# A written order for the expert stage, and a block product accumulated on a copy of another

## The chip, the cores and the metric

One core of a Trainium2 chip runs the whole kernel. Times are device microseconds (us) of one execution. The median of three runs of the kernel before is 1386.89 us (1381.55 to 1387.7).

## The reference

Three layers follow one another; all data is float32.

```
attn:    q averaged over pairs of rows; softmax(q k^T / sqrt(64)) v;  2 x 8 heads, 1152 rows of k and v, 576 of q
gated:   x = (sigmoid(x @ w_gate) * (x @ w_val)) @ w_out            1152 tokens, 512 -> 1536 -> 512
experts: P = exp(x @ w_gate - max), 8 times scaled to row sums and column sums (1152 x 8)
         out = sum over e of P[:, e] * (relu(x @ w1[e]) @ w2[e])    8 experts, 512 -> 1024 -> 512
```

The change concerns the third layer, called the expert stage here.

## The kernel before, in words

The kernel multiplies on TensorE (PE) in single-precision words of which only the upper part counts. So each operand is split into a high part (ScalarE, ACT: a rounding copy) and a low part (VectorE, DVE: value minus high part), and a product is three matmuls: high by high, high by low, low by high (`three`, L789). Matrix products of the expert stage are made from 2 x 2 blocks in seven block products instead of eight. The seven use the blocks A11, A12, A22 of one operand and four sums of its blocks, S1 to S4; B11 to B22 and T1 to T4 are those of the other. Results of several block products are added, partly in PSUM and partly on DVE.

An expert is done in two halves of 512 hidden columns, so there are sixteen halves. In a half:

- Two first products (`first_product`, L1053), called mi 0 and mi 1, each give 256 hidden columns for all 1152 tokens. A block product has 2 x 6 matmuls of 288 columns into a pair of PSUM banks. `tap` (L1080) copies such a pair to SBUF on ACT, `add` (L1085) adds a pair to a block on DVE and then applies the relu on ACT. GpSimd (POOL) forms S1 to S4 of the hidden values (`join`, L1095), and each of the seven blocks is split (`split`, L1090). 128 of the 1152 tokens stay outside the blocks: `late` (L1126) splits them as the rest.
- One second product (`second_product`, L1152) multiplies these with w2: seven block products of 24 matmuls of 256 columns, and `plain`, 12 matmuls of 512 columns for the rest, in fifth place. After each block product DVE adds four pieces to the result in SBUF (`take`, L1139), scaled by the routing weight of the tokens.

Weights come by DMA in pieces of 512 KB; POOL forms the sums of their blocks (L1006), ACT the high parts (L1011) and DVE the low parts (L1012). `routing` (L937) computes P in the first three halves; its steps are queued behind certain matmuls.

The first block product A11 is needed twice. Before, it is copied to SBUF and goes on in its banks; the next one that belongs to it, A12, begins in banks of its own, and DVE adds it:

```
        product(A11, lambda u: xa[u][:, 0], "a", True)
        mark = tap(h11, "a")
        ...
        product(A12, lambda u: xb[u][:, 0], "b", True)
        add(h11, "b")
```

In the second product the A11 part is taken by DVE in the same way, in four takes, and A12's in four more.

The order of the work: the attention stage has its own list (`arrange`, L180). Each step carries a due time, durations and the buffers that it gets and frees; the list is simulated, each step is placed as early as its inputs and buffers allow, and every engine gets the resulting order. The expert stage has none. Its instructions are ordered by the compiler's scheduler, its PSUM tiles come from a pool of six banks and one of two, and its buffers from rotating pools. Each engine takes its queue in order.

Ahead of the expert stage, `combine_x0` (L887) and `combine_x1` (L899) form the blocks of x from the output of the gated stage.

Of the kernel before, what the change touches and what calls it, by code (L numbers as in the profile page):

```python
# [16 lines left out]
P = 128  # L17
# [3 lines left out]
RT0 = 24  # L21
# [4 lines left out]
AHEAD = 8.0  # L26


@with_exitstack
def moe_stack_kernel(ctx: ExitStack, tc: tile.TileContext, q, k, v, wg1, wv1, wo1, wg2, w1, w2, out):  # L30
# [96 lines left out]

    HALF = (0, 2 * P), (2 * P, SP - 2 * P)
    U = 2 * QT + 1

    with ExitStack() as pa:
# [40 lines left out]
        def step(name, eng, when, takes, lasts, emit, deps=(), takes_buf=(), frees=(), after=()):  # L172


            steps[name] = dict(
                name=name, eng=eng, when=when, takes=takes, lasts=lasts, emit=emit, deps=(*deps, *after),
                after=after, gets=takes_buf, frees=frees, seq=len(steps),
            )

        def arrange():  # L180

            wake = dict(PE=145, ACT=80, DVE=40, POOL=140, SP=100)
            users, need, ready = {}, {}, {e: [] for e in wake}
            for s in steps.values():
                need[s["name"]] = len(s["deps"])
                s["at"] = 0.0
                for d in s["deps"]:
                    users.setdefault(d, []).append(s)
                if not s["deps"]:
                    ready[s["eng"]].append(s)  # L190
            idle = {kind: [(0.0, k) for k in range(len(t))] for kind, t in stock.items()}
            line = sorted(steps.values(), key=lambda s: (s["when"], s["seq"]))
            turn = {kind: [s["name"] for s in line if any(k == kind for k, _ in s["gets"])] for kind in stock}
            given, front, free, out = {}, 0, dict.fromkeys(wake, 0.0), []
            begun = set()
            while len(out) < len(steps):
                while line[front]["name"] in begun or line[front]["eng"] == "SP":
                    front += 1
                limit, best = line[front]["when"] + AHEAD, None
                for eng, queue in ready.items():  # L200
                    for s in queue:
                        if s["when"] > limit and eng != "SP":
                            continue
                        t = max(free[eng], s["at"])
                        for kind, _ in s["gets"]:
                            if not idle[kind] or (kind != "g" and turn[kind][0] != s["name"]):
                                break
                            t = max(t, min(idle[kind])[0] + wake[eng])
                        else:
                            key = t, s["when"], s["seq"]  # L210
                            if best is None or key < best[0]:
                                best = key, s
                (t, _, _), s = best
                ready[s["eng"]].remove(s)
                begun.add(s["name"])
                free[s["eng"]] = t + s["takes"]
                for kind, what in s["gets"]:
                    slot = min(idle[kind])
                    idle[kind].remove(slot)
                    if kind != "g":  # L220
                        turn[kind].pop(0)
                    given[what] = kind, slot[1]
                s["got"] = [(what, *given[what]) for _, what in s["gets"]]
                for what in s["frees"]:
                    kind, k = given[what]
                    idle[kind].append((t + s["lasts"], k))
                for u in users.get(s["name"], ()):
                    own = s["lasts"] + wake[u["eng"]]
                    if s["name"] in u["after"] or u["eng"] == s["eng"] in ("PE", "POOL"):
                        own = s["takes"]  # L230
                    u["at"] = max(u["at"], t + own)
                    need[u["name"]] -= 1
                    if not need[u["name"]]:
                        ready[u["eng"]].append(u)
                out.append((t, len(out), s))
            return [s for _, _, s in sorted(out, key=lambda x: x[:2])]
# [542 lines left out]
        with tc.manual_schedule(engines=engines):  # L779
            for s in arrange():  # L780
                for what, kind, slot in s["got"]:
                    have[what] = stock[kind][slot]
                s["emit"]()
# [114 lines left out]

    def combine_x1():  # L899
# [5 lines left out]
        x3 = misc.tile([P, N], F32, tag="m", name="xs")  # L905
        x22, x21 = (x3[:, n * HT:(n + 1) * HT] for n in range(2))
# [4 lines left out]
        t3 = misc.tile([P, N], F32, tag="m", name="t3")[:, 0:HT]  # L911
        nc.vector.tensor_tensor(out=t3, in0=x22, in1=x12_, op=ALU.subtract)
        split_x(xc[1][:, 1], t3)
        yield
        split_x(xb[1][:, 1], x22)
        nc.gpsimd.tensor_tensor(out=x21, in0=x21, in1=x11, op=ALU.subtract)
        split_x(x12[:, 1], x12_, nc.gpsimd)
        split_x(xd[:, 1], x21, nc.gpsimd)
# [7 lines left out]
    x2_done = []  # L926
    pbs.close()
    ps_f = ctx.enter_context(tc.tile_pool(name="ps_f", bufs=6, space=PSUM, reuse_waits="tile"))
    ps_y = ctx.enter_context(tc.tile_pool(name="ps_y", bufs=2, space=PSUM, reuse_waits="tile"))

    HW = 4 * P
    tokens = [HT + t * P for t in range(4)] + [t * P for t in range(4)]

    def two(x):
        return x.rearrange("p (n w) -> p n w", n=2)

    def routing():  # L937

        lg = pr
        yield  # L940

        ltr = misc.tile([P, N], F32, tag="m", name="lt")[0:2 * E]
        for n in range(2):
            for nb in range(2):
                pl = ps_f.tile([P, 512], F32, tag="f", name="pl")
                cols = slice(nb * HB, (nb + 1) * HB)
                for c in range(KD):
                    u, h = divmod(c, 2)
                    x = ((x12[:, u], xb[u][:, 1]), (xa[u][:, 0], xb[u][:, 0]))[n][h]
                    nc.tensor.matmul(  # L950
                        pl[0:2 * E, 0:HB], wgs[:, c].rearrange("p s e -> p (s e)"), x[:, 0, cols],
                        start=(c == 0), stop=False,
                    )
                    nc.tensor.matmul(
                        pl[0:E, 0:HB], wgs[:, c, 0], x[:, 1, cols], start=False, stop=(c == KD - 1),
                    )
                for c0, c1, t0 in ((0, HB, 0),) if nb == 0 else ((0, HW - HB, HB), (HW - HB, HB, 2 * HW - n * (2 * HW - HT))):
                    t0 += n * HW
                    nc.scalar.activation(out=ltr[:, t0:t0 + c1 - c0], in_=pl[0:2 * E, c0:c1], func=AF.Copy)
        pt = ps_y.tile([P, 512], F32, tag="y", name="plt")  # L960
        yield
        for t in range(NT):
            c0 = (t + 4) % 8 * P if t < 8 else t * P
            nc.tensor.transpose(
                pt[:, t * 2 * E:(t + 1) * 2 * E], ltr[:, c0:c0 + P], ident[0:2 * E, 0:2 * E]
            )
        both = pt[:, 0:NT * 2 * E].rearrange("p (t s e) -> p t s e", s=2, e=E)
        nc.scalar.activation(out=lg, in_=both[:, :, 0], func=AF.Copy)
        nc.vector.tensor_tensor(out=lg, in0=both[:, :, 1], in1=lg, op=ALU.add)
        mx = rt.tile([P, 1], F32, tag="mx", name="mx")  # L970
        nc.vector.tensor_reduce(out=mx, in_=lg, axis=AX.XY, op=ALU.max)
        yield
        pmx = ps_y.tile([P, 512], F32, tag="y", name="pmx")
        nc.tensor.transpose(pmx[:, 0:P], mx.to_broadcast([P, P]), ident)
        ngm = rt.tile([P, 1], F32, tag="ngm", name="ngm")
        nc.vector.tensor_reduce(out=ngm, in_=pmx[:, 0:P], axis=AX.X, op=ALU.max, negate=True)
        nc.scalar.activation(out=pr, in_=lg, func=AF.Exp, bias=ngm)
        for _ in range(8):
            rs = rt.tile([P, NT, 1], F32, tag="rs2", name="rs2")
            nc.vector.tensor_reduce(out=rs, in_=pr, axis=AX.X, op=ALU.add)  # L980
            nc.vector.tensor_scalar(out=rs, in0=rs, scalar1=1e-9, scalar2=None, op0=ALU.add)
            nc.vector.reciprocal(out=rs, in_=rs)
            nc.vector.tensor_tensor(out=pr, in0=pr, in1=rs.to_broadcast([P, NT, E]), op=ALU.mult)
            cs = rt.tile([P, 1, E], F32, tag="cs", name="cs")
            nc.vector.tensor_reduce(out=cs[:, 0], in_=pr.rearrange("p t e -> p e t"), axis=AX.X, op=ALU.add)
            yield
            pc = ps_y.tile([P, 512], F32, tag="y", name="pc")
# [292 lines left out]
```

## Time and profile before

| | |
|---|---|
| median of runs | 1386.89 us |
| profiled execution | 1389.38 us |
| its span | 1387.6 us |
| PE busy | 1281.8 us (92%) |
| DVE busy | 1114.7 us (80%) |
| ACT busy | 777.8 us (56%) |
| POOL busy | 721.5 us (52%) |
| mean granted clock of PE | 0.968 |

The span runs from the first to the last instruction. Busy times of PE include the modelled ends of pipelined matmuls, which overlap, so a busy PE is not PE at its peak; the distance between the starts of matmuls says how fast it runs. The granted clock is a share of 2.4 GHz. An engine's idle time is put down to what ended it.

### The profile page before, as it was taken

To read this page: it belongs to the slowest core of one execution; us is meant where nothing else is said; L and a number is where in the kernel's file an instruction comes from. 1 tells how busy PE (TensorE), PEld (TensorE's weight loads), DVE (VectorE), ACT (ScalarE), POOL (GpSimd) and SP (SyncE) were. 2 spreads that over 40 slices of the span, in tenths; PEclk is the share of its full clock that TensorE was granted. 3 is DMA by queue.
4 is the path that set the end of the run, shared out by engine and by line. 5 is a ranking of instruction groups with operands and counts; after the bars stand their busy time and mean duration, and the time that the engine had idled before them with its cause. 6 is when DMAs were issued, how large, how long until landed. Compare 5 with 4: busy or idle time off the path is not lost.

```text
span 1387.6 us, 23795 instructions
## 1 busy us (share of the span) xinstructions
PE 1281.8 (92%) x8922; PEld 1240.0 (89%) x8922; DVE 1114.7 (80%) x2083; ACT 777.8 (56%) x1708; POOL 721.5 (52%) x751
## 2 busy tenths in 40 slices
PE   8999999989999997989899899899899899899898
PEld 7889999989999996979789889889889889889887
DVE  7999999986566648998878878878888978888776
ACT  7999999943343226463454554554554654554542
POOL 6788887653444226443544544444445544445441
PEclk9999999999999997999999999999999999999999
DMA  5111210122222211111011011111111111011101
GB/s 154 35 52 52 61 36 20 54 63 89 92 80 89 91 46 61 34 44 32 31 46 47 31 46 47 31 47 47 31 46 47 31 46 47 31 46 47 31 1 69
DMA packets 61204, 70.50 MB, mean 51 GB/s; under 512 B 3360, under 2 KB 47776, under 8 KB 61088
## 3 DMA queue, kind: packets, MB, share of 16 engines
q1 hardware_dynamic: 61088, 68.97, 16.1%
q8 instruction: 70, 1.15, 0.4%
q14 instruction: 46, 0.38, 0.1%
HBM read 66.60 MB, written 2.36 MB: 50 GB/s over the span
## 4 chain that ended last, share of the span: by engine, by line
PE 58%; DVE 17%; ACT 12%; POOL 7%; issue 5%; DMA 1%; SPq 0%; DVEq 0%; ACTq 0%; POOLq 0%
POOL hs L1097 7%; PE psb L792 5%; PE psb L791 4%; PE psb L790 4%; ACT hb L1092 4%; PE pya L1169 4%; PE pya L1175 3%; PE pya L1176 3%; DVE hb L1093 3%; DVE pT L410 3%; PE psa L790 3%; PE psa L792 2%; PE psa L791 2%; PE psg L429 2%; DVE w_w L1012 2%
## 5 line engine op out<-in xcount | busy, mean ns | idle before, releaser
L1006 POOL TENSOR_TENSOR sm_w<-raw_w 128x256 f32<-128x256 f32 x128 | 108.7, 849 | 356.0 <-DVE w_w L1012 287.9
L1011 ACT ACTIVATE w_w<-sm_w 128x512 fp32r<-128x512 f32 x128 | 78.5, 626 | 156.6 <-PE pyc L1176 72.2
L1169 PE MATMUL pya<-w_w,hb 128*128 128x256 f32 x512 | 146.9, 287 | 16.1 <-DVE acc L1148 15.9
L1093 DVE TENSOR_TENSOR hb<-hs,hb 128x512 fp32r<-128x512 f32 x128 | 119.8, 955 | 37.2 <-ACT hb L1092 36.5
L1175 PE MATMUL pya<-w_w,hb 128*128 128x256 f32 x512 | 144.9, 283 | 0.0
L1176 PE MATMUL pya<-w_w,hb 128*128 128x256 f32 x512 | 144.7, 283 | 0.0
L790 PE MATMUL psa<-xc,w_w 128*128 128x288 f32 x256 | 86.5, 338 | 51.6 <-ACT hr L1082 51.6
L429 PE MATMUL psg<-pT,vs 128*128 128x256 f32 (+1 forms) x576 | 133.1, 318 | 0.2
L1092 ACT ACTIVATE hb<-hs 128x512 fp32r<-128x512 f32 x128 | 76.9, 624 | 93.9 <-POOL hs L1097 93.8
L1097 POOL TENSOR_TENSOR hs<-hr 128x512 f32<-128x512 f32 x64 | 86.4, 1370 | 67.3 <-ACT hr L1088 67.3
L1011 ACT ACTIVATE w_w<-raw_w 128x512 fp32r<-128x512 f32 (+1 forms) x128 | 73.2, 573 | 81.0 <-PE py L1190 43.6
L1169 PEld LDWEIGHTS pya<-w_w,hb 128*128 128x128 f32 x512 | 96.8, 189 | 19.9 <-DVE acc L1148 18.8
L410 DVE TENSOR_TENSOR pT<-psg,pT 128x384 fp32r<-128x384 f32 x192 | 102.0, 551 | 7.4 <-ACT pT L406 5.5
L1012 DVE TENSOR_TENSOR w_w<-raw_w,w_w 128x512 fp32r<-128x512 f32 (+1 forms) x128 | 103.9, 821 | 4.4 <-ACT w_w L1011 3.4
L790 PEld LDWEIGHTS psa<-xc,w_w 128*128 128x128 f32 x256 | 56.1, 219 | 55.7 <-ACT hr L1082 55.7
L390 PE MATMUL psg<-ident,p 128*128 128x128 f32 x648 | 104.4, 273 | 0.9 <-DVE pT L410 0.3
L1012 DVE TENSOR_TENSOR w_w<-sm_w,w_w 128x512 fp32r<-128x512 f32 x128 | 98.2, 769 | 6.3 <-ACT w_w L1011 6.3
L792 PE MATMUL psb<-x,w_gv 128*128 128x384 f32 x288 | 97.6, 339 | 3.6 <-POOL w_gv L120 3.6
L1175 PEld LDWEIGHTS pya<-w_w,hb 128*128 128x128 f32 x512 | 97.2, 190 | 0.7
L1176 PEld LDWEIGHTS pya<-w_w,hb 128*128 128x128 f32 x512 | 97.5, 190 | 0.2
L790 PE MATMUL psb<-x,w_gv 128*128 128x384 f32 x288 | 97.4, 338 | 0.0
L791 PE MATMUL psb<-x,w_gv 128*128 128x384 f32 x288 | 97.3, 338 | 0.0
(235 smaller groups left out, 4783.5 us busy)
## 6 DMA issues: line engine op xcount, KB each, us to landing
raw_w<-in_moe_w_dram SPq DMA_DIRECT2D x64, 512.0 KB, 3.5
raw_gv<-in_moe_w_gate_dram SPq DMA_DIRECT2D x12, 512.0 KB, 3.6
raw_gv<-in_moe_w_val_dram SPq DMA_DIRECT2D x12, 512.0 KB, 3.6
raw_o<-in_moe_w_out_dram SPq DMA_DIRECT2D x12, 512.0 KB, 3.4
vr<-in_v_dram SPq DMA_DIRECT2D x16, 288.0 KB, 2.8
kr<-in_k_dram SPq DMA_DIRECT2D x15, 288.0 KB, 2.8
qr<-in_q_dram SPq DMA_DIRECT2D x15, 256.0 KB, 3.7
out_dram<-acc SPq DMA_DIRECT2D x8, 256.0 KB, 2.2
```

Source lines behind the costliest of these rows:

```text
L410: nc.vector.tensor_tensor(out=lo, in0=turned(i, u, g), in1=f(hi), op=ALU.subtract)
L429: nc.tensor.matmul(have["pv", i, j, n][:, 0:HALF[n][1]], have["vs", i, j][:, jj].rearrange("p a d -> p (a d)"), have["pT", i, j, n][s][:, ...
L790: nc.tensor.matmul(ps, wh, xh, start=first, stop=False, skip_group_check=more)
L791: nc.tensor.matmul(ps, wh, xl, start=False, stop=False, skip_group_check=more)
L792: return nc.tensor.matmul(ps, wl, xh, start=False, stop=last, skip_group_check=more).ins
L1011: nc.scalar.activation(out=w[:, 0], in_=src, func=AF.Copy)
L1012: nc.vector.tensor_tensor(out=w[:, 1], in0=src, in1=f(w[:, 0]), op=ALU.subtract)
L1093: nc.vector.tensor_tensor(out=h[:, 1], in0=src[:, 0:HW], in1=f(h[:, 0]), op=ALU.subtract)
L1097: nc.gpsimd.tensor_tensor(out=t, in0=a[:, 0:HW], in1=b[:, 0:HW], op=op)
L1169: ins = nc.tensor.matmul(out_, h[:, 0, cols], w[:, 0], start=(first and k + m == 0), stop=False, skip_group_check=True,).ins
L1175: nc.tensor.matmul(out_, h[:, 0, cols], w[:, 1], start=False, stop=False, skip_group_check=True)
L1176: nc.tensor.matmul(out_, h[:, 1, cols], w[:, 0], start=False, stop=(m == 1), skip_group_check=True)
```

## The change

The expert stage gets a list of steps like that of the attention stage. `arrange` becomes a function of the whole kernel and is told, in addition, which steps of DVE and POOL are not to be placed at the same time (`port`), when buffers are free at first, and that a buffer with several users is free after the last. The written due times repeat every 45.4 us a half; a table SHIFT moves single kinds of steps against them. All five engines get the resulting order.

The eight PSUM banks become four fixed pairs, X, Y, B and y. In both products ACT copies A11 from its pair to pair B, A12 is accumulated there, and only the sum is read: by ACT with the relu in the first product, by DVE in four takes in the second. So that PE may add to banks that ACT has written, two matmuls (`ready_banks`) write pair B once at the start. `plain` moves from fifth to second place. Weights, splits, sums, takes and routing compute what they did before.

```diff
-    ps_f = ctx.enter_context(tc.tile_pool(name="ps_f", bufs=6, space=PSUM, reuse_waits="tile"))
-    ps_y = ctx.enter_context(tc.tile_pool(name="ps_y", bufs=2, space=PSUM, reuse_waits="tile"))
+    ps_f = ctx.enter_context(tc.tile_pool(name="ps_f", bufs=1, space=PSUM, reuse_waits="tile"))
...
-        mark = tap(h11, "a")
...
-        product(A12, lambda u: xb[u][:, 0], "b", True)
-        add(h11, "b")
...
+SHIFT = {
+    "go 0": 8888, "go 0 0": 2522, "go 0 1": -12434, "go 1": 9837, "go 1 0": 1123, "go 1 1": 11151, "hh 0 0": 8968,
...
+    def arrange(steps, stock, ahead, begin=None, held=None):
+
+        wake = dict(PE=145, ACT=80, DVE=40, POOL=140, SP=100)
...
+        line = sorted(steps.values(), key=lambda s: (s["when"], s["seq"]))
+        turn = {kind: [s["name"] for s in line if any(k == kind for k, _ in s["gets"])] for kind in stock}
+        given, front, free, out = dict(held or {}), 0, dict.fromkeys(wake, 0.0), []
+        port, until = 0.0, {}
+        begun = set()
...
+            limit, best = line[front]["when"] + ahead, None
+            for eng, queue in ready.items():
+                for s in queue:
+                    if s["when"] > limit and eng != "SP":
+                        continue
+                    t = max(free[eng], s["at"], port if s["port"] else 0.0)
+                    for kind, _ in s["gets"]:
+                        if not idle[kind] or (kind != "g" and turn[kind][0] != s["name"]):
+                            break
+                        t = max(t, min(idle[kind])[0] + wake[eng])
+                    else:
+                        key = t, s["when"], s["seq"]
+                        if best is None or key < best[0]:
+                            best = key, s
...
+            for what in s["frees"]:
+                kind, k = given[what]
+                until[what] = max(until.get(what, 0.0), t + s["lasts"])
+                hold[what] -= 1
+                if not hold[what]:
+                    idle[kind].append((until[what], k))
...
+    stock = {
+        "raw": [rawp.tile([P, 1024], F32, tag="raw", name="raw_w") for _ in range(3)],
+        "cv": [conv.tile([P, 512], F32, tag=t, name="sm") for t in ("da", "da", "ds", "ds", "dv", "dv")],
+        "w1": [w_p.tile([P, 2, 1, 2, P], F32R, tag=f"w1{k}", name="w_one") for k in range(2)],
+        "w2": [w_p.tile([P, 2, 2, 2, P], F32R, tag=f"w2{k}", name="w_two") for k in range(9)],
+        "h": [h_p.tile([P, 2, HW], F32R, tag="h", name="hb") for _ in range(13)],
+        "hp": [hp_p.tile([P, 2, 2, HT - HW], F32R, tag="hp", name="hp") for _ in range(4)],
+        "m": [spare[0], xs[2], xs[1], spare[1]],
+    }
+    bank = {f"{k}{n}": ps_f.tile([P, 512], F32, tag=f"{k}{n}", name=f"ps{k}") for k in "XYBy" for n in range(2)}
+    acc = o_p.tile([P, NT, DM], F32, tag="acc", name="acc")
...
+    def step(name, eng, when, takes, lasts, emit, deps=(), gets=(), uses=(), after=(), port=False, least=0.0, ps=""):
...
+        key = name if isinstance(name, str) else " ".join(map(str, (name[0], *name[2:])))
+        entry(
+            steps, name, eng, when * 1e3 + SHIFT.get(key, 0), takes, lasts, emit, deps, list(gets), [*dict.fromkeys(uses)], list(after),
+            port, least * 1e3,
+        )
...
+    START, PERIOD, PHASE = 14.0, 45.4, 11.25
...
+    def split(name, o, src, deps, when, uses=()):
+
+        tile_ = ("h", *name, o)
+        step(
+            ("hh", *name, o), "ACT", when, 530, 630, lambda: copy(have[tile_][:, 0], src()), deps,
+            [("h", tile_)], [tile_, *uses],
+        )
+        step(
+            ("hl", *name, o), "DVE", when + 0.7, 600, 690,
+            lambda: join(nc.vector, have[tile_][:, 1], src(), f(have[tile_][:, 0]), ALU.subtract),
+            [("hh", *name, o)], (), [tile_, *uses], port=True,
+        )
+
...
+        product(0, A11, lambda u: xa[u][:, 0], a, True)
+        for nb in range(2):
+            step(
+                ("go", *name, nb), "ACT", tf + 0.8 * (nb + 1), 295, 410,
+                lambda nb=nb: copy(bank[f"B{nb}"][:, 0:HB], bank[f"{a}{nb}"][:, 0:HB]), ps=f"{a}{nb} B{nb}=",
+            )
+        product(1, S1, lambda u: xa[u][:, 1], c, True)
+        tap("t22", 1, c, 1, 1, get=True)
+        product(2, S2, lambda u: xc[u][:, 0], a, False)
+        tap("t21", 2, a, 0, 1, get=True)
+        product(3, A12, lambda u: xb[u][:, 0], "B", False)
+        tap("r11", 3, "B", 0, 0, AF.Relu)
+        r11 = [("r11", *name, nb) for nb in range(2)]
+        product(4, S3, lambda u: xc[u][:, 1], a, False)
+        add("r22", 4, a, 1, 1, "t22")
+        product(5, S4, lambda u: xb[u][:, 1], c, False, [f"xl{0}"])
+        add("r21", 5, c, 0, 1, "t21")
+        product(6, A22, lambda u: xd[:, u], a, False, [f"xl{2}"])
+        tap("r12", 6, a, 1, 0, AF.Relu)
+        routing((*name, 7))
+        r12 = [("r12", *name, nb) for nb in range(2)]
+        r22, r21 = ("r22+", *name), ("r21+", *name)
...
+        product(0, A11, B11, a, True)
+        for n in range(2):
+            step(
+                ("go", hx, n), "ACT", ts + 1.44 * (n + 1), 530, 640, lambda n=n: copy(bank[f"B{n}"], bank[f"{a}{n}"]),
+                ps=f"{a}{n} B{n}=",
+            )
+        step(
+            ("p", hx), "PE", ts + SLOT, 2800, 3100, plain,
+            [("pl", hx, m, i) for m in range(2) for i in range(2)] + [("wl", hx, m, 2, i) for m in range(2) for i in range(2)],
+            (), [("hp", hx, m, i) for m in range(2) for i in range(2)] + [("w", hx, m, 2, i) for m in range(2) for i in range(2)],
+            ps="y0=",
+        )
+        step(
+            ("tk", hx, "p"), "DVE", ts + 2 * SLOT, 650, 750, lambda: take(e, half, NT - 1, slice(0, DM), bank["y0"], True),
+            ps="y0",
+        )
+        finish(NT - 1, 1, ("tk", hx, "p"))
+        product(2, S1, T1, c, True)
+        takes(2, S1, c, 4, 1, True)
+        product(3, S2, T2, a, False)
+        takes(3, S2, a, 0, 1, True)
+        product(4, A12, B21, "B", False)
+        takes(4, A12, "B", 0, 0, True)
+        product(5, S3, T3, a, False)
+        takes(5, S3, a, 4, 1, False)
+        product(6, S4, B22, c, False)
+        takes(6, S4, c, 0, 1, False, True)
+        product(7, A22, T4, a, False)
+        routing((hx, 2, 8))
+        takes(7, A22, a, 4, 0, True, True)
...
+    def ready_banks():
+        x = xa[0][:, 0, 0]
+        for n in range(2):
+            nc.tensor.matmul(bank[f"B{n}"], x[:, 0:P], x[:, 0:512], start=True, stop=True)
...
+    step("set", "PE", START - 1, 460, 700, ready_banks, ps="B0= B1=", least=START - 1)
+    for hx in range(2 * E):
+        for mi in range(2):
+            first_product(hx, mi)
+        second_product(hx)
+    begin = {("w2", k): 4000.0 + 1000 * k for k in range(3, 9)}
+    engines = {nc.tensor.engine, nc.vector.engine, nc.scalar.engine, nc.gpsimd.engine, nc.sync.engine}
+    with tc.manual_schedule(engines=engines):
+        for s in arrange(steps, stock, 30e3, begin, {("x", 0): ("m", 0), ("x", 1): ("m", 1)}):
+            for what, kind, slot in s["got"]:
+                have[what] = stock[kind][slot]
+            s["emit"]()
```

## Rows read from the trace of the kernel before

**Rows 1.** Busy us (instructions) of PE, PEld, DVE, ACT, POOL by stretch, clock, DMA share, GB/s

```profile
50.00:250.00 200.00, 198.58 (x1460) 187.36 (x1460) 189.24 (x428) 185.70 (x501) 160.95 (x225) 1.00 0.16 45
...
699.80:1330.50 630.70, 571.32 (x4178) 556.99 (x4177) 512.77 (x901) 326.11 (x673) 306.42 (x289) 0.96 0.13 40
```

**Rows 2.** Timeline of PE: start us, length us, engine, line, operation, idle before

```profile
518.74 0.29 PE L790 MATMUL psa<-xa,w_w 128*128 128x288 f32 x1
...
699.76 0.30 PE L790 MATMUL psa<-xa,w_w 128*128 128x288 f32 x1
...
1138.58 0.61 PE L790 MATMUL psa<-xc,w_w 128*128 128x288 f32 x1 [3.24 <-ACT hr L1082]
...
1162.04 0.39 PE L1188 MATMUL py<-w_w,hp 128*128 128x512 f32 x1
...
1164.85 0.28 PE L1169 MATMUL pya<-w_w,hb 128*128 128x256 f32 x1
...
1173.48 0.30 PE L790 MATMUL psa<-xa,w_w 128*128 128x288 f32 x1
...
1184.63 0.29 PE L790 MATMUL psa<-xa,w_w 128*128 128x288 f32 x1
...
1330.52 0.29 PE L790 MATMUL psa<-xa,w_w 128*128 128x288 f32 x1
...
1382.68 0.27 PE L1176 MATMUL pya<-w_w,hb 128*128 128x256 f32 x1
```

**Rows 3.** Waits of PE, 699.8 to 1330.5: total us, times, longest us

```profile
PE psa L790 <- ACT hr L1082: 38.9, 12, 3.2
PE pya L1169 <- DVE acc L1148: 14.2, 12, 1.5
PE pyc L1176 <- DVE hb L1093: 6.2, 7, 1.6
```

**Rows 4.** The chain of waits, 1120 to 1145: start us, us, what

```profile
1134.29 1.73 POOL hs L1097
...
1136.04 2.19 ACT hb L1092 x4
...
1138.23 0.30 ACT hr L1082
...
1139.19 0.24 PE psa L791
```

**Rows 5.** Durations ns by line, 699 to 1331 (min/median/max); last row by form, 300 to 430

```profile
L1087 DVE TENSOR_TENSOR hr<-psb,hr x48: 450/458/460, 705.6 to 1300.7; 128x288 f32<-128x288 f32 x48
...
L1148 DVE SCALAR_TENSOR_TENSOR acc<-pya,pr,acc x195: 463/471/485, 698.5 to 1330.7; 128x256 f32<-128x256 f32 x195
...
L1082 ACT ACTIVATE hr<-psa x144: 382/406/414, 700.8 to 1306.1; 128x288 f32<-128x288 f32 x144
...
L107 ACT ACTIVATE dv_gv<-raw_gv 128x512 f32<-128x512 f32 x19 | 12.1, 637 | 16.3 <-DVE ds_gv L117 15.0 <-DMA raw_gv<-in_moe_w_val_dram 1.3
```

**Rows 6.** Timeline of DVE, then durations by line, 699 to 1331

```profile
1134.80 1.36 DVE L1134 TENSOR_TENSOR hp<-hr,hp 128x128 fp32r<-128x128 f32 x1
...
L1012 DVE TENSOR_TENSOR w_w<-raw_w,w_w x97: 424/685/1233, 699.3 to 1330.1; 128x512 fp32r<-128x512 f32 x73, 128x256 fp32r<-128x256 f32 x24
...
L1134 DVE TENSOR_TENSOR hp<-hr,hp x48: 275/706/1376, 712.1 to 1315.1; 128x128 fp32r<-128x128 f32 x48
...
L1006 POOL TENSOR_TENSOR sm_w<-raw_w x97: 732/738/1197, 698.6 to 1329.4; 128x256 f32<-128x256 f32 x97
...
L1097 POOL TENSOR_TENSOR hs<-hr x48: 1282/1344/1742, 711.3 to 1307.2; 128x512 f32<-128x512 f32 x48
```

**Rows 7.** Timeline of PE at the start of the expert stage

```profile
521.17 0.37 PE L790 MATMUL psa<-xa,w_w 128*128 128x288 f32 x1 [1.48 <-DVE xs L907]
...
525.89 0.61 PE L792 MATMUL psc<-xa,w_w 128*128 128x288 f32 x1 [3.29 <-DVE w_w L1012]
```

## What I predict

> **What bounds the kernel now.** I began with the busy time by stretch [rows 1]. The change touches only the expert stage, so the first question is what share of the span that is and which engine is full there. In twelve half experts (699.8 to 1330.5) PE is busy 571.32 of 630.7 us, DVE 512.77, ACT 326.11, POOL 306.42, and the granted clock averages 0.96 of its higher level, 2.4 GHz. So PE is the fullest engine, but it neither runs all the time nor always at the full clock.
>
> Next I read the timeline of PE to get a floor, by starts of matmuls and not by their modelled ends [rows 2]. One half expert consists of two first products and a second one. 84 matmuls of 288 columns go from 1173.48 to 1184.63: 11.15 us. The second product has 168 matmuls of 256 columns and 12 of 512. The 12 go from 1162.04 to 1164.85 (2.81 us), the next 72 of 256 columns from there to 1173.48 (8.63 us, 0.120 each), so 168 take 20.14. The floor of a half is 2 x 11.15 + 20.14 + 2.81 = 45.25 us. What it takes: the half that begins at 699.76 and the one at 1330.52 are twelve apart, 52.56 us each, 7.3 over the floor. Expert work starts at 518.74 and its last matmul at 1382.68, some 1382.95 with its end. Three parts lie over the floor: the first three halves 181.0 - 3 x 45.25 - 7.7 = 37.5 us (7.7 is routing's PE work, under *Rest*), twelve halves 87.7, the last 7.2. Together 132 us; no change that leaves the matmuls alone can win more.
>
> The waits of PE in those twelve halves [rows 3] say who makes it wait: ACT's copies of a product out of PSUM 38.9 us (12 times, up to 3.2), DVE's takes of the second product 14.2, DVE's low parts 6.2: 59.3 us, 4.9 a half. The rest, 7.3 - 4.9 = 2.4 us a half, is the clock: a granted mean of 0.96 [rows 1] is 4% of 52.56, 2.1 us. After the 3.24 us stall at 1138.58 [rows 2] the matmuls come 0.24 us apart instead of 11.15 / 84 = 0.133, which is the 1.2 GHz level [rows 4].
>
> The chain of waits [rows 4] says why ACT is late. ACT's short copy at 1138.23 stands behind four splits of sums (2.19 us), these behind POOL's sums, of which one from 1134.29 took 1.73. ACT takes its queue in order: a copy that PE needs and that could have run at once waits some 3 us behind splits that nobody needs yet. This is a matter of order; ACT is only 52% busy.
>
> **The change part by part.**
>
> *First block product.* Before, the first product's first block is copied out, the next block product goes to its own banks, DVE adds the two and ACT applies the relu. Now ACT copies bank to bank, PE accumulates on the copy, and ACT applies the relu on the way out. DVE loses 2 adds for each first product, 4 a half at 458 ns [rows 5]: 1.8 us. ACT loses one relu of 576 columns (some 0.7, scaled from the 0.637 of 512 in rows 5) and gains two reads of 288 (0.41 each): +0.2 us a half. PE's work is the same.
>
> *Second product.* The four takes of its first block go: DVE -4 x 0.471 = -1.9 us a half. ACT gains two copies of 512 columns from PSUM to PSUM. No row has that operation. From below the 0.406 us of 288 columns out of PSUM, from above the 0.637 of 512 columns into PSUM [rows 5]; I take 0.637, the row with the same width, so +1.3 us a half. ACT then stands at 27.2 + 0.2 + 1.3 = 28.7 us of 45.25 (63%). The copy is needed four slots (11.5 us) later in the second product and three (4.8 us) in the first; it lies beside matmuls and costs PE nothing unless ACT is over 3 us late again.
>
> *The order.* All engines get one written order, from a list that starts each step as soon as its inputs and buffers are there. So the copy that PE waits for no longer stands behind the splits, the unsplit rest of the second product moves from fifth to second place, which gives the splits of the sums 2.8 us more, and four fewer takes free the banks earlier. All three waits of rows 3 are aimed at, and with the stall the slow clock goes. How well such a list holds on the chip is seen in the attention stage, which before already runs from one: in 50 to 250 PE is busy 198.58 of 200 us at clock 1.00 with DVE at 189 and ACT at 186 [rows 1]. That is 0.7% idle beside engines fuller than any here. 0.7% of a half is 0.3 us.
>
> *What is late next.* DVE and POOL. DVE had 512.77 / 12 = 42.7 us a half and keeps 39.0, 86% of the floor. POOL's work is unchanged. But the two exclude one another: a low part of 128 columns, 0.275 us at the least, took 1.36 us from 1134.80 [rows 6] and ended just behind POOL's sum of 1134.29 [rows 4], at 1136.1; of 48 adds with one operand in PSUM none took over 0.46 us [rows 5]. So what DVE does from SBUF alone and what POOL does must follow each other. With the undisturbed durations of rows 6 (0.685, the median, for the 28 low parts of 512 columns, the least for the others) a half has 28 x 0.685 + 2 x 0.42 + 4 x 0.28 = 21.1 us of such DVE work and 16 x 0.73 + 8 x 1.28 = 21.9 us of POOL: 43.0 of 45.25, 95%. That fits, but barely, so I do not give the attention stage's 0.3 us but 1.0 us of loss for each of the last 15 halves; bounds 0.1 and 3 (3 is the longest wait that rows 3 show, once a half). The Trainium skill (SBUF — State Buffer, SBUF: two separate sides) says the same of the port pair that VectorE and GpSimd share: an exclusive lock held for the whole instruction, the loser blocks fully, and a VectorE operation with two SBUF inputs takes part. By that rule no order can run the two at once; the trace agrees (1.36 us against 0.275).
>
> *The start.* Before, the first six expert matmuls begin at 518.74, right behind the stage before, then PE waits for DVE's read of the last output banks (to 521.17) and 3.29 us for a weight [rows 7]. Now a new step writes the copy banks first (2 matmuls, 0.5 us), and by their place in the pools I take these to be the banks that DVE reads last. PE then does nothing from 518.74 to 521.17, 2.4 us, and the clock may fall for it: another 2.4, the price found above. For the weights I take the 3.3 us of before, for the eight routing turns and the x parts still to be made 5 us (before, the first three halves lost 37.5 over the floor, against 22 for three usual ones, so 15 more than usual; half of that rounds to 8, of which 3.3 are the weights). Together 13; bounds 5 (weights ready, no clock lost) and 25 (nothing gained there).
>
> *Rest.* Routing does the same operations: 32 matmuls of 288 columns at 0.133, and 26 small ones that I count at 0.13 too, an estimate from rows 2: 7.7 us. Attention and the gated stage have the same instructions. Behind the last matmul lie 4.65 us of takes and stores to the end at 1387.6; the same now.
>
> **The sum.** 518.74 + 16 x 45.25 + 7.7 + 0.5 + 13 + 15 x 1.0 + 4.65 = 1283.6 us of span. The profiled execution took 1389.38 for its span of 1387.6, 1.8 around it: 1285.4. The median of the runs is 1386.89, 2.5 under the profiled one, hence 1283; I say 1284. Its own range: 5 at the start and 0.1 a half give 1262, 25 and 1.4 a half 1302.
>
> **Rivals.**
>
> A, *DVE and POOL become the bound.* 95% leaves 2.2 us a half; if exclusion and order leave more than that unused, PE waits for low parts. For it: a list written from durations can't follow a POOL sum that takes 1.28 to 1.74 us [rows 6]. Against it: DVE's work on PSUM (takes, adds) can fill POOL's time. 3 us a half instead of 1: 1284 + 15 x 2 = 1314.
>
> B, *slower than before.* In a fixed order on every engine a late POOL sum holds up ACT's next split, and with it the copies behind it, as rows 4 show for one first product a half. If the list places a split just ahead of the copies in both first products, and POOL is late by the lock, each costs 3.24 us of stall and 2.4 of clock; with the (14.2 + 6.2) / 12 = 1.7 us of other waits that is 13.0 a half: 1284 + 15 x 12.0 = 1464. It decides from 8.3 us a half (132 / 16), where the result is that of before. For it: that ACT stalls so now. Against it: the copies are ready earlier than the splits, and the list starts what is ready first.
>
> C, *the order does half of what it says.* The ACT stall goes, but the waits for takes and low parts come back elsewhere: 5 us a half, 1284 + 15 x 4 = 1344.
>
> D, *no change.* The 7.3 us are latency of the chain product, sum, split, low part, and not queue order; 1387. Against it: the copy that PE waits for reads a product that is done and needs nothing of that chain, and PE waits so 12 times in 24 first products, not in each.
>
> **Chances.** Forecast 0.66, A 0.18, C 0.09, B 0.05, D 0.02. The range takes in the forecast's own and most of A: 1262 to 1325. Half a per cent, 7 us, is about what can be told from no change: faster 0.93 (forecast, A, C), same 0.02 (D), slower 0.05 (B).
>
> **What would show it.** Starts of halves some 46.3 us apart in the changed kernel's timeline; granted clock 1.00 from the second half on; no wait of PE for ACT's copies above 1 us; DVE near 39 and ACT near 29 us a half. If A holds, PE waits for DVE's low parts, these take far more than the 0.685 of rows 6, and DVE or POOL is full. If the halves are 45.5 apart, my 1.0 was too much; if PE starts before 520, the bank step is not where I put it. Wrong is all of it if the halves stay above 50 us apart.

## The result and the profile after

The changed kernel takes 1289.14 us (median of 4 runs, 1287.63 to 1292.6), before 1386.61 beside it: ratio 0.9307, interval 0.9278 to 0.9337. The forecast was 1284, its range 1262 to 1325. The profiled execution has a span of 1285.4 us.

The busy time of twelve halves of the changed kernel, in the columns of [rows 1]:

```profile
680.96:1235.71 554.75, 546.17 (x4178) 537.16 (x4177) 483.53 (x804) 326.38 (x720) 320.01 (x289) 1.00 0.15 47
```

Twelve halves take 554.75 us where they took 630.7, 46.23 each, at a mean granted clock of 1.00. PE's matmuls are the same 4178. DVE is busy 40.3 us a half (42.7 before, 39.0 forecast), ACT 27.2 as before (28.7 forecast), POOL 26.7 (25.5 before).

PE's timeline, the answer to [rows 2] and [rows 7] (start, length, engine, operation, idle before):

```profile
522.41 1.19 PE L1380 MATMUL psB<-xa 128*128 128x512 f32 x2 [7.44 <-DVE xs L955]
...
680.96 0.30 PE L835 MATMUL psY<-xa,w_two 128*128 128x288 f32 x1
...
1136.02 0.38 PE L1281 MATMUL psX<-w_two,hb 128*128 128x256 f32 x1 [0.68 <-DVE acc L1239]
...
1235.71 0.29 PE L835 MATMUL psY<-xa,w_two 128*128 128x288 f32 x1
...
1280.86 0.27 PE L1286 MATMUL psY<-w_two,hb 128*128 128x256 f32 x1
```

The first row is the writing of the copy banks: PE waits 7.44 us for it, and expert work starts at 523.40. In the half from 1097.13 the starts of matmuls show one gap only, before the row at 1136.02: 0.93 us, the whole distance of that half from the floor of 45.25.

The waits of PE from 518 on, to set beside [rows 3] (total us, times, longest):

```profile
PE psB L1380 <- DVE xs L955: 7.4, 1, 7.4
PE psX L1281 <- DVE acc L1239: 5.1, 7, 1.0
PE psy L1472 <- DVE cs L1425: 4.2, 2, 2.3
PE psY L1281 <- DVE acc L1239: 4.1, 6, 0.7
PE psX L835 <- ACT psB L1018: 2.0, 1, 2.0
```

ACT's wait, 38.9 us in twelve halves before, is gone but for one of 2.0 at the start. What is left in each half is a wait for DVE's take. DVE's timeline shows why it is late:

```profile
1130.61 0.86 DVE L1239 SCALAR_TENSOR_TENSOR acc<-psX,pr,acc 128x256 f32<-128x256 f32 x2
1131.39 1.11 DVE L1021 TENSOR_TENSOR hb<-sm,hb 128x512 fp32r<-128x512 f32 x1
1132.42 1.22 DVE L1021 TENSOR_TENSOR w_two<-sm,w_two 128x512 fp32r<-128x512 f32 x1
1133.57 1.22 DVE L1021 TENSOR_TENSOR hb<-sm,hb 128x512 fp32r<-128x512 f32 x1
1134.71 0.47 DVE L1239 SCALAR_TENSOR_TENSOR acc<-psB,pr,acc 128x256 f32<-128x256 f32 x1
1135.11 0.86 DVE L1239 SCALAR_TENSOR_TENSOR acc<-psX,pr,acc 128x256 f32<-128x256 f32 x2
```

POOL runs beside all three low parts:

```profile
1131.21 0.74 POOL L1021 TENSOR_TENSOR sm<-raw_w,sm 128x256 f32<-128x256 f32 x1
1131.90 1.20 POOL L1021 TENSOR_TENSOR sm<-raw_w 128x256 f32<-128x256 f32 x1
1133.18 1.07 POOL L1021 TENSOR_TENSOR sm<-sm,raw_w 128x256 f32<-128x256 f32 x1
1134.20 1.87 POOL L1021 TENSOR_TENSOR sm<-raw_w 128x256 f32<-128x256 f32 x2
```

The bank that PE wants at 1135.1 is read from 1135.11 on, behind three low parts of 1.1 to 1.2 us (0.685 is the median of [rows 6]). The third of them can come later, as `e9_move` shows below.

At the start ACT and DVE show this:

```profile
515.07 0.63 ACT L1018 ACTIVATE w_two<-sm 128x512 fp32r<-128x512 f32 x1 [12.07 <-PE pso L837]
...
516.30 0.76 DVE L114 TENSOR_TENSOR xc<-xs,xc 128x576 fp32r<-128x576 f32 x1 [11.92 <-ACT xc L113]
...
520.92 1.34 DVE L955 COPY xs<-pso 128x1152 f32<-128x1152 f32 x1
```

A high part of a weight sum stands in ACT's queue ahead of the x blocks and waits 12.07 us, until the gated stage's last matmul. The x blocks wait behind it, DVE behind them, and DVE reads the last output banks only from 520.19 to 522.26, though the gated stage's last matmul ended at 515.0.

### The profile page after: what moved, and what is told of

Its sections match the earlier page's. It is cut to its first block, busy times and chain, and to the rows that moved or that the text cites. A ratio compares the mean times of both kernels' runs of the same rounds, so it can differ in the third digit from the quotient of the medians.

```text
span 1285.4 us, 23682 instructions
## 1 busy us (share of the span) xinstructions
PE 1244.3 (97%) x8924; PEld 1210.1 (94%) x8924; DVE 1074.5 (84%) x1955; ACT 779.6 (61%) x1772; POOL 737.6 (57%) x751
## 3 DMA queue, kind: packets, MB, share of 16 engines
q8 instruction: 70, 1.15, 0.4%
## 4 chain that ended last, share of the span: by engine, by line
PE 65%; DVE 26%; ACT 6%; issue 2%; DMA 1%; POOL 0%; SPq 0%; DVEq 0%; ACTq 0%; POOLq 0%
DVE hb L1021 9%; DVE acc L1239 4%; PE psb L837 4%; PE psb L836 4%; PE psb L835 4%; PE psY L835 4%; PE psY L837 4%; PE psY L836 4%; PE psX L835 4%; PE psX L837 4%; PE psX L836 4%; DVE pT L455 3%; PE psg L474 3%; PE psg L435 2%; PE psY L1281 2%; PE psX L1281 2%
## 5 line engine op out<-in xcount | busy, mean ns | idle before, releaser
L1021 POOL TENSOR_TENSOR sm<-raw_w 128x256 f32<-128x256 f32 x128 | 120.0, 952 | 81.9 <-DMA raw_w<-in_moe_w_dram 52.7
L1021 DVE TENSOR_TENSOR hb<-sm,hb 128x512 fp32r<-128x512 f32 x128 | 128.0, 1010 | 39.5 <-ACT hb L1018 39.5
L1281 PE MATMUL psY<-w_two,hb 128*128 128x256 f32 x384 | 109.2, 284 | 5.0 <-DVE acc L1239 4.1
L1281 PE MATMUL psX<-w_two,hb 128*128 128x256 f32 x384 | 109.0, 284 | 5.1 <-DVE acc L1239 5.1
L1018 ACT ACTIVATE w_two<-sm 128x512 fp32r<-128x512 f32 x128 | 80.8, 631 | 51.1 <-POOL sm L1021 34.3
L1286 PE MATMUL psX<-w_two,hb 128*128 128x256 f32 x384 | 108.3, 282 | 0.0
L1286 PE MATMUL psY<-w_two,hb 128*128 128x256 f32 x384 | 108.2, 282 | 0.0
L1285 PE MATMUL psY<-w_two,hb 128*128 128x256 f32 x384 | 108.2, 282 | 0.0
L1285 PE MATMUL psX<-w_two,hb 128*128 128x256 f32 x384 | 108.1, 282 | 0.0
L1021 DVE TENSOR_TENSOR w_two<-sm,w_two 128x512 fp32r<-128x512 f32 x128 | 94.7, 749 | 2.4 <-ACT w_two L1018 0.6
L1018 ACT ACTIVATE hb<-sm 128x512 fp32r<-128x512 f32 x128 | 78.5, 626 | 29.9 <-POOL sm L1021 27.8
L474 PEld LDWEIGHTS psg<-pT,vs 128*128 128x128 f32 x576 | 91.1, 189 | 3.7 <-DVE pT L455 0.7
L451 ACT ACTIVATE pT<-psg 128x384 fp32r<-128x384 f32 x192 | 90.6, 499 | 5.9 <-PE psg L435 4.6
L1021 POOL TENSOR_TENSOR sm<-raw_w,sm 128x256 f32<-128x256 f32 x96 | 84.2, 884 | 3.7
```

The lines of the kernel that those rows point to most:

```text
L451: nc.scalar.activation(out=p_parts(i, u, g)[0], in_=turned(i, u, g), func=AF.Copy)
L474: nc.tensor.matmul(have["pv", i, j, n][:, 0:HALF[n][1]], have["vs", i, j][:, jj].rearrange("p a d -> p (a d)"), have["pT", i, j, n][s][:, ...
L1018: nc.scalar.activation(out=out_, in_=in_, func=func)
L1021: eng.tensor_tensor(out=out_, in0=a, in1=b, op=op)
L1281: nc.tensor.matmul(out_, h[:, 0, cols], w[:, 0], start=(begins and kk + m == 0), stop=False, skip_group_check=True,)
L1285: nc.tensor.matmul(out_, h[:, 0, cols], w[:, 1], start=False, stop=False, skip_group_check=True)
```

## The experiments

**The two parts apart.** `e1_no_copy` keeps the list and undoes the copy in both products:

```diff
-            step(("go", *name, nb), "ACT", ... copy(bank[f"B{nb}"][:, 0:HB], bank[f"{a}{nb}"][:, 0:HB]) ...)
+        tap("t11", 0, a, 0, 0, get=True)
...
-        product(3, A12, lambda u: xb[u][:, 0], "B", False)
-        tap("r11", 3, "B", 0, 0, AF.Relu)
+        product(3, A12, lambda u: xb[u][:, 0], "B", True)
+        add("r11", 3, "B", 0, 0, "t11")
...
-            step(("go", hx, n), "ACT", ... copy(bank[f"B{n}"], bank[f"{a}{n}"]) ...)
+        takes(0, A11, a, 0, 0, True)
...
-        product(4, A12, B21, "B", False)
-        takes(4, A12, "B", 0, 0, True)
+        product(4, A12, B21, "B", True)
+        takes(4, A12, "B", 0, 0, False)
```

> The written order kept, the copy undone in both products: the first block goes to SBUF, the next one starts in pair B, DVE adds (4 adds, 4 takes more a half, about 3.7 us of DVE work, none of it from SBUF alone). Theory 'the order did it': DVE goes from 40.3 to about 44 us a half, still under 46.2; halves 46 to 47.5 us apart, 1290 to 1310. Rival 'the copy did it, by relieving DVE': halves 49 us or more apart, 1335 or more.

1308.87 us, ratio 0.9457 (0.9428 to 0.9486). From the fourth on the halves are 46.93 us apart (46.20 with the copy). The first theory's times hold; its 44 us of DVE came out as 41.6, in part because the low parts of 512 columns took 0.85 us on average here and 0.90 with the copy. The whole kernel loses 20 us without the copy: 0.7 us in each later half, and more in the first three. These 20 us are not the copy's alone: the table SHIFT stayed, but the list placed the other steps anew around it, and a table made for this list was not tried.

`e2_copy_only` puts the copy into the kernel before, in the compiler's order, with `plain` still in fifth place. Shown are the banks and the first product; the second product is changed in the same way:

```diff
-    ps_f = ctx.enter_context(tc.tile_pool(name="ps_f", bufs=6, ...))
+    ps_f = ctx.enter_context(tc.tile_pool(name="ps_f", bufs=4, ...))
+    pair = [ps_2.tile([P, 512], F32, tag=f"B{n}", name="psb") for n in range(2)]
...
+        for nb in range(2):
+            mark = nc.scalar.activation(out=pair[nb][:, 0:HB], in_=ps["a"][nb][:, 0:HB], func=AF.Copy).ins
```

> The kernel before with the copy alone: pair B fixed, four rotating banks for the other products, the compiler's order. Theory 'the order did it': ACT's stall of about 3.2 us a half stays, only the waits for DVE's takes shrink; halves 51 to 53 us apart, 1360 to 1390. Rival 'the copy did it': halves under 49, 1330 or less.

1356.74 us, ratio 0.9798 (0.9766 to 0.9831); twelve halves 50.65 us apart on average, both just under what I expected. DVE is busy 37.3 us a half (third busy time of the first line), and PE's first wait is ACT still (whole expert stage):

```profile
691.30:1299.15 607.85, 569.96 (x4179) 551.92 (x4177) 447.88 (x805) 330.44 (x721) 293.54 (x289) 0.97 0.13 42
PE psa L790 <- ACT psb L1109: 32.2, 16, 3.9
PE py L1198 <- DVE hp L1140: 13.2, 14, 1.2
```

The stall is where it was, on the copy this time. DVE is 5.4 us a half less busy and the halves gain 1.9: DVE's load was not the bound.

**Is it the list, or its table?** `e5_no_shift` has `SHIFT = {}`, `e6_no_port` also this:

```diff
-                    t = max(free[eng], s["at"], port if s["port"] else 0.0)
+                    t = max(free[eng], s["at"])
```

> The changed kernel with the table SHIFT empty: the list goes by the due times as written. Theory 'the list itself removes ACT's stall, the table only arranges DVE and POOL': no wait of PE for ACT above 1 us, halves 47 to 49.5 us apart, 1300 to 1340. Rival 'without the table the list is no better than the compiler's order': halves 51 us or more.

> As the run with the empty table, and the list no longer told that DVE's work from SBUF alone and POOL's exclude one another. Theory 'what the chip excludes, the list must know': 1 to 2 us a half more than with the empty table alone, 15 to 30 us. Rival 'the engines sort it out in their queues': the same within 5 us.

1410.09 us, ratio 1.0182 (1.0152 to 1.0212): slower than before. And 1413.08 (1.0206, 1.0167 to 1.0246): whether the list knows of the exclusion makes 3 us with the table empty, no more than the two intervals leave open, and the halves are 54.6 us in the mean either way. With the table filled this was not tried. The waits of PE in `e5_no_shift`:

```profile
PE psY L1252 <- DVE xs L992: 25.7, 8, 3.5
PE psX L1252 <- DVE t L992: 24.6, 7, 3.5
PE psX L1256 <- DVE w_two L992: 21.0, 18, 4.8
PE psY L1256 <- DVE w_two L992: 16.2, 20, 1.5
```

The wait for ACT is gone, as the theory said, but halves are 54.0 to 55.4 us apart, as the rival said. PE now waits for DVE's adds (`xs`, `t`), which stand behind low parts in DVE's queue, and for low parts, and with these stalls the granted clock is 0.94 (700 to 1300). Neither theory named what happens: the list alone takes the stall from ACT to DVE.

**The start.** `e3_start` queues the step that waits 12 us behind the last ACT instruction of the first x blocks:

```diff
+            with tc.issue_after(mark) if s["name"] == ("wh", 0, 0, 1, 2) else ExitStack():
                 s["emit"]()
```

> The changed kernel, but ACT's first high part of a weight sum (and what follows it in the list) is queued behind the ACT work of the first x blocks. Theory 'that step stood ahead of the x blocks and held up DVE's read of the last output banks by 5 us': PE's first wait falls from 7.4 to 2.5 us or less, 1282 to 1285 (5 us and some clock less than the changed kernel's 1289). Rival 'the weights or the x parts are next in line': the wait moves to the first products, 1288 to 1290.

1284.5 us, ratio 0.9283 (0.9253 to 0.9312). That is 4.6 less than the 1289.14, but the intervals of the two ratios overlap, so it is the trace that decides. The first wait is as expected, from the end of the gated stage to the third half it is 116.2 us instead of 119.8, and from there on the halves are unchanged (46.20):

```profile
PE psB L1380 <- DVE xs L955: 2.3, 1, 2.3
```

**The last wait.** `e4_take` tries to get the late take forward by its due times:

```diff
-    "tk 4 1 0": 1909, "tk 4 1 1": 1586
+    "tk 4 1 0": -4000, "tk 4 1 1": -4000
```

> The changed kernel with two entries of SHIFT changed, so that DVE does the takes of S2's second pair of pieces ahead of two splits and a weight. Theory 'the 0.93 us that each half still loses is DVE coming to this take late': halves 45.3 us apart, 15 x 0.9 = 14 us less, 1275. Rival 'DVE and POOL exclude one another, and what is put behind is late instead': PE waits for a low part or another take, halves 46 us or more, 1286 to 1295.

1314.9 us, ratio 0.9505 (0.9478 to 0.9532), more than either theory said. The wait for takes is gone, one for a low part has come, as the rival had it, and from the sixth on the halves are 47.73 apart:

```profile
PE psX L1285 <- DVE w_two L1021: 18.9, 8, 3.4
PE psY L1285 <- DVE w_two L1021: 16.1, 8, 2.5
```

The two entries made the list place other steps elsewhere; a weight's low part now comes behind the takes of the next block product. So `e9_move` leaves the list as it is and only moves the two takes ahead of the one low part that can wait, with the start of `e3_start`:

```diff
+            late = [at["tk", hx, S2, 1, k] for k in range(2)]
+            split_s4 = at["hl", hx, 1, S4]
+            if row.index(split_s4) < row.index(late[0]):
+                row = [s for s in row if s not in late]
+                i = row.index(split_s4)
+                row[i:i] = late
```

> The start of e3_start, and in the finished list the two takes of S2's second pair moved ahead of S4's low part, nothing else. Theory 'the 0.93 us that a half still loses is this take standing behind that low part': no wait of PE for takes, halves 45.3 us apart, 1284.5 - 14 = 1271. Rival 'what is put behind is late in its turn, as in e4_take': PE waits for S4's low part, halves 46.0 or more, 1282 or more.

1271.9 us, ratio 0.9194 (0.9169 to 0.9218), beside `e12_again`, the changed kernel once more, with 1290.66 (0.9324, 0.9302 to 0.9346):

> The changed kernel itself, beside e9_move on one chip: 1289 within 3 us, halves 46.2 us apart, by every theory.

The busy time of `e9_move` between 673 and 1220:

```profile
673.00:1220.00 547.00, 547.00 (x4211) 540.41 (x4210) 488.83 (x815) 326.61 (x721) 322.79 (x289) 1.00 0.15 48
```

PE never stops, and eleven halves from 721.60 to 1219.38 are 45.25 us apart: the floor. So this take was what the halves still lost, and the low part that it now stands ahead of was not needed earlier. It is the best version of this study.

**Which engine has room?** `e7_pool` doubles every second weight sum on POOL, `e8_act` three of four high parts of weights on ACT, each 5.9 us a half with the list told so:

```diff
-            join(nc.gpsimd, *t[x]())
+            for _ in range(1 + x % 2):
+                join(nc.gpsimd, *t[x]())
...
-            copy(have["w", *name, x][:, 0], source(x))
+            for _ in range(1 + (x > 0)):
+                copy(have["w", *name, x][:, 0], source(x))
```

> The changed kernel with every second POOL sum of weights done twice: 8 x 0.73 = 5.9 us more POOL work a half, written over with the same values. Theory 'DVE's work from SBUF alone and POOL's exclude one another, 43.0 of 46.2 us now': the sum is 48.9, halves at least 48.9 us apart, 1330 or more. Rival 'POOL, 26.7 us busy of 46.2, has room': halves 46.2 to 46.8, under 1300.

> The changed kernel with three of four high parts of weights done twice on ACT: 5.9 us more ACT work a half, with the same values. Theory 'ACT has room and stands in nobody's way': halves 46.2 to 46.8 us apart, under 1300. Rival 'any engine's lateness goes through in a written order': halves 48 us or more.

1322.3 us (0.9549, 0.9507 to 0.9591) and 1318.07 (0.9519, 0.9476 to 0.9561); halves 47.7 apart with POOL's load, 47.8 to 49.1 with ACT's. POOL's halves fell between its two theories, and the new durations changed the list as well, so load and order are not told apart. So `e10_pool_same` and `e11_act_same` are the same loads with the list's durations, and so the order that it gives, untouched. (Only at the start do the queues differ: in `e11_act_same` the first x blocks come earlier, and PE's first wait is 2.3 us.)

> The POOL load of e7_pool (every second weight sum twice, 5.9 us a half) with the list unchanged: the order is that of the changed kernel. Theory 'DVE and POOL exclude one another and are nearly full together': PE waits for DVE's low parts, halves 47.5 us or more apart. Rival 'the 1.5 us a half of e7_pool came from another order': halves under 46.7.

> The ACT load of e8_act (5.9 us a half) with the list unchanged. Theory 'ACT has room, the 1.6 us and more of e8_act came from another order': halves under 46.7 us apart. Rival 'in a written order the lateness of any engine goes through to PE': halves 47.5 or more, as with the POOL load.

POOL's load: 1293.27 us (0.9343, 0.9305 to 0.9381), halves 46.03 apart from the fourth on. ACT's: 1317.95 (0.9521, 0.9485 to 0.9558), halves 48.20 apart. `e12_again` on the same chip took 1290.66. Busy times of `e10_pool_same` in twelve halves, then its two groups of weights' low parts (busy us, mean ns), then the same two groups of the changed kernel:

```profile
684.00:1239.00 555.00, 548.72 (x4200) 539.73 (x4199) 508.81 (x810) 326.79 (x721) 420.32 (x388) 1.00 0.15 47
```

```profile
L1021 DVE TENSOR_TENSOR w_two<-sm,w_two 128x512 fp32r<-128x512 f32 x97 | 86.1, 897 | 0.0
L1021 DVE TENSOR_TENSOR w_two<-raw_w,w_two 128x512 fp32r<-128x512 f32 x72 | 66.1, 944 | 0.2 <-ACT w_two L1018 0.2
```

```profile
L1021 DVE TENSOR_TENSOR w_two<-sm,w_two 128x512 fp32r<-128x512 f32 x96 | 71.0, 749 | 1.6
L1021 DVE TENSOR_TENSOR w_two<-raw_w,w_two 128x512 fp32r<-128x512 f32 x72 | 49.2, 697 | 2.7
```

POOL is busy 34.9 us a half instead of 26.7, the low parts take 0.90 and 0.94 us where the changed kernel's took 0.75 and 0.70, and in these halves PE notices nothing; only the second and third half are 1.2 and 2.1 us longer than in `e12_again`. For ACT the load costs 27 us here and as much in `e8_act`, so it is not another order that does it. The stretches of one half say why, first products and second product of the changed kernel:

```profile
1097.10:1119.40 22.30, 22.30 (x170) 22.30 (x169) 17.88 (x30) 17.74 (x42) 8.30 (x7) 1.00 0.16 48
1119.40:1143.30 23.90, 23.22 (x182) 22.47 (x181) 22.30 (x38) 9.45 (x19) 18.20 (x18) 1.00 0.15 46
```

ACT is busy 80% of the first products and 40% of the second. In `e11_act_same` it is 21.06 of 23.0 us in the first products, and PE waits there for its copies (the wait for takes has grown as well):

```profile
1119.00:1142.00 23.00, 22.07 (x167) 21.84 (x166) 16.52 (x28) 21.06 (x48) 9.15 (x8) 1.00 0.15 47
PE psX L1282 <- DVE acc L1240: 7.7, 7, 1.1
PE psX L835 <- ACT t L1018: 6.8, 7, 1.3
PE psY L835 <- ACT xs L1018: 6.7, 8, 0.9
```

## Why the prediction was right, and where not

*What bounds the kernel* held: the floor of 45.25 us a half is reached in `e9_move`, and of the 132 us over the floor the change won 97.

*The order* was the larger part: with the list and without the copy 1308.87 us, with the copy and without the list 1356.74. ACT's stall went, and the slow clock with it. `plain` in second place counts to the order here; no run takes it apart from the list. But the reason I gave failed: that a list which starts each step as soon as its inputs and buffers are there holds on the chip, as in the attention stage. Without the table of shifts that list gives 1410, slower than before. The table is worth 121 us, and I passed over it. My rival B (0.05) had the mechanism, a late step that holds up what stands behind it, but on ACT; it came true on DVE in `e5_no_shift`.

*What is late next.* I took 1.0 us a half and measured 0.95 to 0.98, which was luck, for the reason was wrong. I read 43.0 of 45.25 us of exclusive DVE and POOL work as nearly full, and rival A rested on that. The sum was too high: with the 5.9 us of the POOL load it would be 48.9, and the halves of `e10_pool_same` are 46.03. Counted in the timelines, DVE from SBUF alone or POOL, at least one of them, runs for 38.6 of 46.2 us in the changed kernel and for 42.9 of 46.0 in `e10_pool_same`. One reason is that I added recorded lengths, and these overlap at their ends: the three low parts above start 1.03 and 1.15 us apart, and the first two last 1.11 and 1.22. Whether that is the whole difference is not shown. So there was room, and `e9_move` reaches the floor with the full exclusive load. The exclusion made three low parts some 0.4 to 0.5 us longer ahead of one take, but what it cost hung on one place in the order. It is also part of why DVE came to 40.3 us and not 39.0: takes and adds fell as priced, but the low parts add up to 28.8 us a half, 28.1 before. Why more POOL work took 0.17 us off a half is open.

*ACT's room.* I had 63% as an average over the half. In the first products ACT is 80% busy, and the 3.3 us that `e11_act_same` adds there already make PE wait; an average over stages misled here as it would over the kernel. The load that I added for the copies was right: the lengths of ACT's instructions add up to 31.7 us a half, 30.1 before, 1.6 more where I had 1.5. The copy bank to bank took 0.58 us for 512 columns, where I had taken 0.637, and 0.39 for 288. That the busy time still stayed at 27.2 comes from how it is counted: the ends of instructions that follow one another overlap and count once, and they overlap more than before.

*The start* was mis-sized. From the end of the gated stage at 515.0 to the third half at 634.77 are 119.8 us; less two floors, 7.7 of routing, 0.5 for the bank step and 0.95 of the second half that is 20, not 13. The bank step waits where I put it, but 7.44 us and not 2.4, for the step on ACT that I had not seen coming; `e3_start` takes the wait to 2.3. The weights, for which I had 3.3 us, made PE wait for nothing. Routing took 4.2 us of waits, ACT's first copies and the x blocks 2.4, and some 6 us are left for the slow clock, of which I had 2.4; from 525 to 545 the mean granted clock is 0.85.

*The sum* of the span, 1283.6 for 1285.4, came out near because errors cancelled: +7 at the start, -1 in the halves, and -3.7 because the gated stage ended at 515.0 and not at 518.7 (below). Most of the 5 us between 1284 and 1289.14 lies outside it: I took the median of the runs 2.5 us under the profiled execution, as before, and it was 1.5 above.

## What to carry to other kernels

A written order is worth what its details are: the same kernel gave 1410, 1315, 1289 and 1272 us by its order alone. Find the one instruction in front of the late one in the finished list and move that; a changed due time or duration makes the list place everything anew. And judge an engine's room in the stretch in which it is waited for.

## What the runs showed of the hardware

The gated stage begins in every kernel with the same wait of PE for its first weight (before, then after):

```profile
291.48 0.69 PE L792 MATMUL psb<-x,w_gv 128*128 128x384 f32 x1 [3.65 <-POOL w_gv L120]
```

```profile
290.39 0.45 PE L837 MATMUL psb<-x,w_gv 128*128 128x384 f32 x1 [3.67 <-POOL w_gv L150]
```

From 290 to 310 the mean granted clock is then 0.83 before and 1.00 after; in `e12_again`, the same program as after, it is 0.86 and in `e3_start` 0.91. From its first to its last matmul the stage takes 231.7 us before, 228.9 after and 231.4 in `e12_again`. So behind one stall of 3.67 us the clock costs nothing or up to 2.8 us, from one execution to the next. That is most of the 3.9 us by which the stage ended earlier (518.9 before, 515.0 after); the rest lay ahead of it, where the stage's first matmul comes at 287.2 before, at 286.1 after, and between 285.1 and 287.8 in all runs. Nothing of this points to the change: in `e2_copy_only`, whose gated stage is that of before, it ends at 515.9. The Trainium skill (TensorE: Matmul & The Clock Gate, What's actually happening) says that the clock gate's window is free-running and not tied to the kernel's start. The trace agrees so far as one program shows means of 1.00 and 0.86 behind one stall.

A DVE instruction from SBUF alone that began while one of POOL's was running ended only behind that: 0.275 us became 1.36 us in [rows 6], and with more POOL work the mean of a low part went from 0.70 to 0.94 us. DVE's takes, with one operand in PSUM, do not show this: in twelve halves of the changed kernel 154 of 288 (those of 256 columns) have POOL beside them for over 0.4 us, and they take 0.471 us on average, the others 0.472.
